# The first phase of a fused mLSTM and mixture-of-experts kernel, rebuilt: half tiles first, loads by need, a tanh gate and half-precision products

## The chip, the cores and the metric

The kernel runs on one core of a Trainium2 chip. The core has five engines with an instruction queue each, worked in order: TensorE (PE, matrix products into the banks of PSUM), VectorE (DVE), ScalarE (ACT), GpSimd (POOL) and SyncE (SP, which issues most of the transfers). The metric is the device time of one execution in microseconds. Before the change it was 260.88 us, the median of three runs (259.86 to 263.05).

## The reference: what is computed

Two stages. The first is an mLSTM recurrence for 4 sequences, 8 heads and 768 steps with 40 x 40 states:

```python
for t in range(S):
    m_new = np.maximum(f_gate[:, :, t] + m, i_gate[:, :, t])
    f_stab = np.exp(f_gate[:, :, t] + m - m_new)
    i_stab = np.exp(i_gate[:, :, t] - m_new)
    C = f_stab * C + i_stab * outer(v_t, k_t)
    n = f_stab * n + i_stab * k_t
    denom = max(abs(n . q_t), 1)
    y[:, :, t] = sigmoid(o_gate[:, :, t]) * (C q_t) / denom
```

The second is a mixture of 8 experts over the 3072 resulting tokens of width 320: logits are `x @ w_gate` plus a bias by the token's modality (two of them), the expert is the largest logit, its weight is the softmax's value there, and the output is that weight times `relu(x @ w1[e]) @ w2[e]` with 1024 hidden units. The inputs are such that the bias decides nearly always, so that all but a few tokens of a modality go to one expert.

## The kernel before

**Two arms.** `still_arm` is a fast way that holds for inputs whose forget gates are high and whose tokens fall into two large classes; guards gathered in `badc` choose the general arm otherwise. Only the fast arm is run here.

**Attention.** The states S of the four sequences after their first 64 steps are built from k and v (`weigh_k`, `state`; the loads are kvs). The tokens behind them are 22 "light" chunks c0 to c21 of 128 tokens: `light` multiplies q (the tile qg, by pairs of chunks, four slots) with S into Y, in 32-bit floats, three products for each span of a chunk. The last two chunks, `special`, are the first 64 steps themselves. For each pair, `sigmoid` turns the output gate og on ACT (exp, ln, exp); `token_rows` multiplies Y with og into xr (DVE), takes the largest absolute value of the denominators, clamps and inverts it (ab), multiplies on POOL, and splits the rows into a high and a low 16-bit part (`rows`: cast on ACT, rest on DVE). `scatter_rows` writes each chunk's rows by an indirect transfer from POOL into x_s, a DRAM array sorted by class A or B.

**Experts.** x_s is worked off in 25 half tiles of 128 tokens, mostly two at a time; the list is STREAM. A tile comes back transposed as xt (`load_tile`, a DMA_TRANSPOSE on SP), once the first NEED chunks are scattered; five slots. The first tile of each class, A0 and B0, does without it: selection products on PE take its rows from the tile `rows` (`select`, L1998). `expert` makes H = w1 x (bank tile H, 64 products a tile in groups of 16, L2070), hh = relu(H) on ACT (L2075), hl = the rest on DVE (L2077), O = w2 (hh + hl) in 24 products a half (L2086), the scaling on ACT and a scatter to the output from POOL. Every weight is used as a high and a low 16-bit half. The weights of A's and B's experts come in 16 pieces through a ring of five `stage` slots (`load_w`, L1823), and each is split by ACT (high, L1824) and DVE (low, L1825).

**What sets the order.** Every operation is an entry in a `Plan` with an engine, an assumed duration, and what it reads and writes. `Plan.run` lists them by their latest start and an assumed cost of each engine and transfer; the resulting order is the program order of every engine. A transfer on SP may not stand earlier than AHEAD less than its latest start. So a changed constant can move instructions on all queues, and what stands ahead of a waiting instruction holds all behind it.

**PSUM.** H0, H1 and H2 are three tiles that take turns for the groups of H; Y0 and Y1 are two halves of one tile Y. A wait is set by tile, not by the half that is used.

Of the kernel before, what the change touches and what calls it, by code (L numbers as in the profile page):

```python
# [1553 lines left out]
def still_arm(tc, a, out):  # L1554
# [174 lines left out]
    def weigh_k(pr):  # L1729
        src = kvs[pr][:, 0:DM].rearrange("p (h d) -> p h d", h=H)  # L1730
        dve(320, lambda: v.tensor_tensor(kw[pr][:, 0:H], src, wT[:, pr * H:(pr + 1) * H].rearrange("p h -> p h ()")
                                         .broadcast_to([P, H, D]), ALU.mult), r=[f"kv{pr}", "wT"], w=[f"kw{pr}"])
# [683 lines left out]
```

## Time and profile before

| | |
|---|---|
| median of three runs | 260.88 us |
| the profiled execution | 260.92 us, span 259.1 us |
| mean granted clock of PE | 0.962 |
| busy: PE, DVE, ACT, POOL | 215.8, 136.9, 92.4, 83.1 us |
| transfers | 31.33 MB, 121 GB/s over the span |
| first product of A0, B0, A1, B1 on H | 27.27, 42.69, 66.32, 82.20 us |
| first scatter into x_s | 36.48 us |
| last expert product | ends at about 247.5 us |

A busy share is an average over stages with different limits, so this page is read by stretches: the start, in which nothing can be multiplied by the experts yet; the first tiles, up to 82 us; the long run of tiles; and the end, in which the last scatters land. A row of a timeline has its start, its length, the engine, the line, the operation, output and inputs, a count, and in brackets how long the engine had been idle and which operation ended that.

### The profile page before, as it was taken

How to read it: one execution, taken by the hardware profiler on the slowest of the kernel's cores; microseconds unless marked ns; L12 is line 12 of the kernel's file. 1: busy time of each engine (PE TensorE's matmuls, PEld its weight loads, DVE VectorE, ACT ScalarE, POOL GpSimd, SP SyncE). 2: the span in 40 equal slices, each digit the busy share in tenths (PEclk: the TensorE clock that was granted, in tenths of full speed). 3: DMA queues.
4: the chain of work that ended last, by engine and by line, in shares of the span. 5: the costliest groups of instructions: out<-in, count | busy, mean ns of one | idle time of the engine just before them, and what ended most of it. 6: DMA issues, size and time to landing. Idle time of an engine off the chain costs nothing.

```text
span 259.1 us, 5180 instructions
## 1 busy us (share of the span) xinstructions
PE 215.8 (83%) x2020; PEld 176.1 (68%) x2020; DVE 136.9 (53%) x422; ACT 92.4 (36%) x161; POOL 83.1 (32%) x99
## 2 busy tenths in 40 slices
PE   0669658746969879999799999999999989999930
PEld 0658536624857758788678788787878758878810
DVE  4666995865680332446997604934151853872200
ACT  1763852853622621318424212322222312312210
POOL 5424338323450030328479561410203031111120
PEclk9999995977999999999999999999999999999995
DMA  5993379999439210144657420163111029301000
GB/s 146 257 293 133 104 215 306 388 218 173 133 103 250 46 52 3 51 108 125 173 159 162 137 89 13 56 154 51 51 28 51 0 36 348 127 15 44 28 10 1
DMA packets 32551, 31.33 MB, mean 121 GB/s; under 512 B 22795, under 2 KB 26285, under 8 KB 32261
## 3 DMA queue, kind: packets, MB, share of 16 engines
q1 hardware_dynamic: 30085, 22.78, 35.5%
q0 software_dynamic: 2432, 8.13, 8.8%
q8 instruction: 17, 0.28, 0.5%
q14 instruction: 17, 0.14, 0.2%
HBM read 18.83 MB, written 8.47 MB: 105 GB/s over the span
## 4 chain that ended last, share of the span: by engine, by line
PE 43%; issue 16%; DVE 16%; DMA 10%; ACT 4%; POOL 4%; SPq 4%; POOLq 0%; DVEq 0%
PE O L2086 20%; PE H L2070 15%; DMA og<-in_ogl 6%; PE Y L1847 5%; POOL out L2096 2%; DVE xr L1862 2%; DVE hl L2077 2%; DMA g_d<-G 2%; DMA x_s<-rows,pos_i 2%; DVE rows L1871 1%; PE Y L1935 1%; DMA sp<-in_spq 1%; SPq L1971 1%; DVE w2lB L1825 1%; DVE w2lA L1825 1%
## 5 line engine op out<-in xcount | busy, mean ns | idle before, releaser
L2077 DVE SCALAR_TENSOR_TENSOR hl<-H,hh 128x512 f16<-128x512 f32 x50 | 34.1, 687 | 59.6 <-ACT hh L2075 59.6
L2086 PEld LDWEIGHTS <-hh 128*128 128x128 f16 x400 | 39.0, 99 | 27.3 <-issue 13.3
L2096 POOL DMA_INDIRECT out<-ob,ois x25 | 24.5, 982 | 89.2 <-ACT ob L2095 86.2
L2070 PE MATMUL H<-xt,w1hB 128*128 128x256 f16 (+1 forms) x320 | 48.1, 257 | 1.1 <-DVE hl L2077 0.8
L2075 ACT ACTIVATE hh<-H 128x512 f16<-128x512 f32 x50 | 29.7, 595 | 52.4 <-PE H L2070 51.3
L2070 PE MATMUL H<-xt,w1hA 128*128 128x256 f16 (+1 forms) x280 | 43.3, 257 | 2.2 <-DVE hl L2077 2.2
L2070 PE MATMUL H<-xt,w1lB 128*128 128x256 f16 (+1 forms) x192 | 42.5, 256 | 0.7 <-DVE w1lB L1825 0.7
L2070 PE MATMUL H<-xt,w1lA 128*128 128x256 f16 (+1 forms) x168 | 38.0, 257 | 2.6 <-DVE w1lA L1825 2.6
L1878 POOL DMA_INDIRECT x_s<-rows,pos_i x24 | 26.9, 1120 | 24.8 <-issue 7.6
L2086 PE MATMUL O<-w2lB,hh 128*128 128x320 f16 x104 | 29.4, 305 | 5.5 <-DVE w2lB L1825 5.3
L2070 PEld LDWEIGHTS <-w1hB 128*128 128x128 f16 x320 | 29.8, 101 | 4.3 <-issue 1.0
L2086 PE MATMUL O<-w2hB,hh 128*128 128x320 f16 x104 | 29.5, 305 | 2.0 <-ACT ob L2095 1.6
L2095 ACT ACTIVATE ob<-O,facs 128x320 f32<-128x320 f32 x25 | 12.8, 525 | 47.7 <-PE O L2086 40.7
L2086 PE MATMUL O<-w2lA,hh 128*128 128x320 f16 x96 | 26.9, 302 | 3.3 <-DVE w2lA L1825 3.3
L1867 POOL TENSOR_TENSOR xr<-xr,ab 128x640 f32<-128x640 f32 x12 | 17.9, 1488 | 36.3 <-DVE ab L1865 27.2
L2070 PEld LDWEIGHTS <-w1hA 128*128 128x128 f16 x280 | 25.7, 98 | 4.9 <-issue 2.4
L2086 PE MATMUL O<-w2hA,hh 128*128 128x320 f16 x96 | 26.7, 301 | 0.1
L1847 PE MATMUL Y<-S,qg 120*128 120x123 f32 (+2 forms) x144 | 22.7, 329 | 4.0 <-DVE xr L1862 2.7
L2086 PEld LDWEIGHTS <-hl 128*128 128x128 f16 x200 | 19.4, 100 | 9.1 <-DVE hl L2077 1.4
L1847 PEld LDWEIGHTS Y<-S,qg 120*128 120x128 f32 (+2 forms) x144 | 21.2, 230 | 5.8 <-DVE xr L1862 3.0
L2070 PEld LDWEIGHTS <-w1lB 128*128 128x128 f16 x192 | 19.2, 100 | 2.3 <-DVE w1lB L1825 0.9
L2070 PEld LDWEIGHTS <-w1lA 128*128 128x128 f16 x168 | 16.4, 98 | 4.4 <-DVE w1lA L1825 3.1
(171 smaller groups left out, 258.1 us busy)
## 6 DMA issues: line engine op xcount, KB each, us to landing
qg<-in_ql SPq DMA_DIRECT2D x11, 360.0 KB, 7.3
og<-in_ogl SPq DMA_DIRECT2D x12, 320.0 KB, 7.3
stage<-in_w SPq DMA_DIRECT2D x8, 384.0 KB, 9.6
stage<-in_w SPq DMA_DIRECT2D x8, 320.0 KB, 10.6
stage<-in_w1t SPq DMA_DIRECT2D x1, 1280.0 KB
og<-in_w SPq DMA_DIRECT2D x1, 1280.0 KB
kvs<-in_kvs SPq DMA_DIRECT2D x2, 364.5 KB, 3.6
sp<-in_spq SPq DMA_DIRECT2D x4, 160.0 KB
```

The costliest lines, as they stand in the source:

```text
L1825: dve(n, lambda hi=hi, lo=lo, sv=sv: v.scalar_tensor_tensor(lo, sv, WSC, hi, ALU.mult, ALU.subtract), r=[f"stage{k}", key + "h"], w=[key + ...
L1847: t_.matmul(y[p0:p1, HQ * g:HQ * g + w], lhsT=q[0:k, i, g, p0:p1], rhs=Ss[b][0:k, g, 0:w], start=(g == 0), stop=(g == 2), skip_group_check ...
L1862: dve(320, lambda h=h: v.scalar_tensor_tensor(x4[:, h], y4[:, h, :, 0:D], XS, og[k][:, h].rearrange("p (h d) -> p h d", h=H), ALU.mult, AL ...
L1867: pool(640, lambda: g_.tensor_tensor(x3, x3, ab.rearrange("p c h o -> p (c h) o").broadcast_to([P, 2 * H, D]), ALU.mult), r=[f"ab{j}"], w= ...
L1871: dve(2 * (z - a0), lambda a0=a0, z=z, o=o: v.tensor_tensor(rows[:, cs, o:o + z - a0], xr[:, :, a0:z], rows[:, cs, a0:z], ALU.subtract), r ...
L1878: ins = g_.indirect_dma_start(out=x_s[:, :], out_offset=bass.IndirectOffsetOnAxis(ap=pos_i[:, c:c + 1].bitcast(U32), axis=0), in_=rows[:, ...
L2070: t_.matmul(hp3[:, i], lhsT=l, rhs=r, start=(i == 0 and q == 0), stop=(i == g - 1 and q == 7), skip_group_check=True)
L2075: act(512, lambda fl=fl, hp3=hp3: s_.activation(hh[:, fl, 0:n], hp3, AF.Relu), r=[nb], w=[f"hh{j}{f}" for f in range(f0, f0 + g)])
L2077: dve(512, lambda fl=fl, hp3=hp3: v.scalar_tensor_tensor(hl[:, fl, 0:n], hp3, 0.0, hh[:, fl, 0:n], ALU.max, ALU.subtract), r=[nb] + [f"hh{ ...
L2086: t_.matmul(op[:, 0:DM], lhsT=t[:, f, P * h:P * h + P], rhs=w[:, f], start=(i == 0), stop=(i == 23))
L2095: act(320, lambda h=h, op=op, o=o: s_.mul(obs[o], op[:, 0:DM], facs[:, s["q0"] + h:s["q0"] + h + 1]), r=[no, f"fac{k}"], w=[f"ob{o}"])
L2096: swdma(164, lambda h=h, o=o: disjoint("outf", g_.indirect_dma_start(out=out[:, :], out_offset=bass.IndirectOffsetOnAxis(ap=ois[:, s["q0"] ...
```

## The change

It has seven parts.

- *Order of tiles and loads.* STREAM begins with four half tiles A0, B0, A1, B1; NEED tells for each tile how many chunks it needs, A1 and B1 now 6 and A2, B2 10. The constants of the planner's costs are new, the stage ring has seven slots, w1 is laid out so that a piece has contiguous rows, the zeros in x_s are stored earlier, and gs is loaded from ACT's queue.
- *Gate.* sigmoid(o) = (tanh(o/2) + 1)/2: one tanh on ACT, and the factor and the 1 go into operations that were there. A second ACT operation sums relu(-tanh(o/2) - 0.98) into `odds`, and the guards send any input with a positive sum to the general arm.
- *Half precision.* From the sixth pair (chunk 10) on, q and S are scaled and split into a high and a low 16-bit half (`halve_q`, Sh and Sl), and a span of Y is nine products of halves in place of three of 32-bit floats.
- *Banks.* H0 and H1 become the two halves of one tile H, and the second pair of chunks uses them as the other pairs use Y (`home`).
- *Rows.* The tile `rows` is a ring of 12 chunks in place of all 24; token numbers are copied into a slot again when it is used a second time, and the guards' sums of the rows are made by pairs.
- *Products of zeros.* 24 products of the tile zrow, 128 x 512, are put on PE where the planner has room.
- *A form.* `tt` makes SCALAR_TENSOR_TENSOR of many TENSOR_TENSOR operations on DVE.

```diff
-    DMA_KB = 230.0
-    AHEAD = 213.0
+    DMA_KB = 320.0
+    AHEAD = 200.0
...
-STREAM = [("A", 0, 1), ("B", 0, 1)]
-for _k in range(1, 6):
+STREAM = [("A", 0, 1), ("B", 0, 1), ("A", 1, 1), ("B", 1, 1)]
+for _k in range(2, 7):
     STREAM += [("A", _k, 2), ("B", _k, 2)]
-STREAM = STREAM[:-1] + [("A", 6, 1), ("B", 5, 2), ("B", 6, 1), ("B", 7, 1)]
-NEED = {1: 7, 2: 12, 3: 16, 4: 20, 5: 24, 6: 24, 7: 24}
+STREAM += [("B", 7, 1)]
+FIRST_HALF = (0, 1, 2, 4, 6, 8, 10, 12)
+NEED = {0: 3, 1: 6, 2: 10, 3: 14, 4: 18, 5: 22, 6: 24, 7: 24}
 NHALF = 25
 SLOTS = 5
+NSTAGE = 7
+WARM = 24
 PRE = 4
-SOON = 25.0
+SOON = 20.0
+RING = 12
+BY_POOL = ()
+PLAIN = 5
+QSC, SSC = 512.0, 256.0
+GATE = 0.98
...
+    def tt(out, x, y, op):
+        return v.scalar_tensor_tensor(out, x, 1.0, y, ALU.mult, op)
...
+    bank = {n: pp.tile([P, 512], F32, name=n) for n in ("H2", "O0", "O1", "M0")}
+    duo = {n: pp.tile([P, 2, 512], F32, name=n) for n in "YH"}
+    for n in "YH":
+        bank.update({n + "0": duo[n][:, 0], n + "1": duo[n][:, 1]})
...
+    rows = tl([P, RING, CW], F16, "rows")
     zrow = tl([P, CW], F16, "zrow")
-    stg = tl([P, 5 * 768], F32, "stage")
-    stage = [stg[:, 768 * i:768 * i + 768] for i in range(5)]
+    stg = tl([P, NSTAGE * 768], F32, "stage")
+    stage = [stg[:, 768 * i:768 * i + 768] for i in range(NSTAGE)]
...
+    dma(16, lambda: s_.dma_start(gs, a["gsp"]), w=["gs"], eng="ACT", bias=-99)
...
+    dve(400, lambda: v.memset(zrow, 0.0), w=["zrow"], bias=-99)
+    for _ in range(WARM):
+        pe(0.3, lambda: t_.matmul(bank["O0"], lhsT=zrow[:, 0:P], rhs=zrow[:, 0:512], start=True, stop=True, skip_group_check=True),
+           r=["zrow"], w=["O0"], bias=500)
...
+        if b:
+            act(3 * HQ, lambda: s_.mul(Sh[b][0:120], Ss[j][0:120], SSC), r=[f"S{j}"], w=[f"Sh{b}"])
+            dve(3 * HQ, lambda: v.scalar_tensor_tensor(Sl[b][0:120], Ss[j][0:120], SSC, Sh[b][0:120], ALU.mult, ALU.subtract),
+                r=[f"S{j}", f"Sh{b}"], w=[f"Sl{b}"])
...
-                src = lambda f0=f0: (a["w1"][ds(regs[c], 1)].rearrange("a p (k f) -> (a p) k f", k=3))[:, :, f0:f0 + 256]
-                sv = st.rearrange("p (k f) -> p k f", k=3)
+                src = lambda i=i: a["w1p"][ds(regs[c], 1), :, 768 * i:768 * i + 768].rearrange("a p f -> (a p) f")
+                sv = st
...
-    def sigmoid(i):
+    def gate(i):
+
         t, k = og[i % 4], f"og{i % 4}"
-        act(640, lambda: s_.activation(t, t, AF.Exp, scale=-1.0), w=[k])
-        act(640, lambda: s_.activation(t, t, AF.Ln, bias=1.0), w=[k])
-        act(640, lambda: s_.activation(t, t, AF.Exp, scale=-1.0), w=[k])
-
-    abss = [small([2, H, 1], f"ab{i}") for i in range(2)]
+        act(640, lambda: s_.activation(t, t, AF.Tanh, scale=0.5), w=[k])
+        act(640, lambda: s_.activation(gjunk.rearrange("p (c d) -> p c d", c=2), t, AF.Relu, bias=gmin, scale=-1.0,
+                                       accum_out=odds[:, i:i + 1]), r=[k, "gmin"], w=["gjunk", f"odd{i}"], bias=15)
...
+    def home(i):
+        return "H" if i == 1 else "Y"
+
+    def halve_q(i):
+        s, d = f"qg{i % 3}", i % 2
+        act(768, lambda: s_.mul(qh[d], qg[i % 3], QSC), r=[s], w=[f"qh{d}"])
+        dve(768, lambda: v.scalar_tensor_tensor(ql[d], qg[i % 3], QSC, qh[d], ALU.mult, ALU.subtract), r=[s, f"qh{d}"], w=[f"ql{d}"])
...
+        if i < PLAIN:
+            r = [f"qg{i % 3}"] + [f"S{b}" for _, _, b in spans(c)]
+            sets = lambda b: [(qg[i % 3], Ss[b])]
+        else:
+            r = [f"qh{i % 2}", f"ql{i % 2}"] + [f"S{x}{b}" for _, _, b in spans(c) for x in "hl"]
+            sets = lambda b: [(qh[i % 2], Sh[b]), (qh[i % 2], Sl[b]), (ql[i % 2], Sh[b])]
...
+                    for e, (q, s) in enumerate(ps):
+                        t_.matmul(y[p0:p1, HQ * g:HQ * g + w], lhsT=q[0:k, j, g, p0:p1], rhs=s[0:k, g, 0:w],
+                                  start=(g == 0 and e == 0), stop=(g == 2 and e == len(ps) - 1), skip_group_check=True)
...
+        for h in range(2):
+            dve(320, lambda h=h: v.scalar_tensor_tensor(x4[:, h], og[k][:, h].rearrange("p (h d) -> p h d", h=H), 1.0,
+                                                        y4[:, h, :, 0:D], ALU.add, ALU.mult), r=Y + [f"og{k}"], w=[f"xr{l}"])
...
+        dve(16, lambda: v.tensor_scalar(ab, ab, one, 2.0 / XS, ALU.max, ALU.mult), w=[f"ab{j}"])
+        dve(40, lambda: v.reciprocal(ab, ab), w=[f"ab{j}"])
...
+        if 2 * i >= RING:
+            dve(2, lambda: v.tensor_copy(rows[:, cs, IDC:IDC + 2].bitcast(I32).rearrange("p c o -> p (c o)"), tok_i[:, 2 * i:2 * i + 2]),
+                r=["cst"], w=[f"id{c0}", f"id{c0 + 1}"])
...
+        dve(640, lambda: v.tensor_reduce(sums[:, 2 * i:2 * i + 2], rows[:, cs, 0:DM], axis=AX.X, op=ALU.add, apply_absolute_value=True),
+            r=[f"rowh{c0}", f"rowh{c0 + 1}"], w=["sums"], bias=15, nb=45 if i < 4 else None)
...
-        swdma(168, scatter, r=[f"rowh{c}", f"rowl{c}", "ids", "rowz", "pos_i", "prefill"], w=[f"xs{c}"])
+        swdma(168, scatter, r=[f"rowh{s}", f"rowl{s}", f"id{s}", "rowz", "pos_i", "prefill"], w=[f"xs{c}"])
...
+        dma(168, lambda: sy.dma_start(x_s[CAP - P:CAP], zrow), r=["zid"], w=["prefill"], nb=8, bias=-60)
+        dma(168, lambda: sy.dma_start(x_s[2 * CAP:2 * CAP + P], zrow), r=["zid"], w=["prefill"], nb=8, bias=-60)
...
-        need = NEED[s["i"]] if s["i"] else 3
+        need = NEED[s["i"]]
...
-                load_q(c // 2) if c < 22 else None
+                if c < 22:
+                    load_q(c // 2)
+                    if c // 2 >= PLAIN:
+                        halve_q(c // 2)
                 load_o(c // 2)
-                sigmoid(c // 2)
+                gate(c // 2)
...
-            chunks((NEED[STREAM[issued][1]] + 1) // 2 * 2)
+            chunks(NEED[STREAM[issued][1]])
```

How the order moves, at three places.

SP, from the fifth piece of weights on, in the kernel before (x_s<-zrow stores zeros, e_i are the experts' numbers):

```order
L1823 DMA stage_88<-in_w2 128x640
L1894 DMA x_s_70<-zrow_87 128x656
L1800 TENSOR_LOAD e_i_150
L1800 ISA x2
L1823 ISA
L1823 DMA stage_88<-in_w2 128x640
L1823 ISA
L1823 DMA stage_88<-in_w2 128x640
L1823 ISA
L1823 DMA stage_88<-in_w2 128x640
L1895 DMA x_s_70<-zrow_87 128x656
```

and in the changed one, from the same piece on:

```order
L1850 DMA stage_90<-in_w2 128x640
L1850 ISA
L1850 DMA stage_90<-in_w2 128x640
L1850 ISA
L1850 DMA stage_90<-in_w2 128x640
L1826 TENSOR_LOAD e_i_159
L1826 ISA x2
L1952 DMA x_s_69<-zrow_89 128x656
L1682 DMA qg0_77<-in_ql 120x768
L1685 DMA og_84<-in_ogl 128x640
L1690 DMA wg_sb_86<-in_wgs 128x24
L1682 DMA qg1_78<-in_ql 120x768
```

Seven pieces now stand in a row with one store of zeros ahead of them, and the second store stands behind the seventh piece, no longer behind the eighth; the next loads of q and og have moved ahead of the eighth piece.

PE from the sorting products (modb) to the first products of q, before:

```order
L1755 LDWEIGHTS ones_120
L1755 MATMUL H2_65<-modb_137,ones_120 128x24
L1756 LDWEIGHTS tri_119
L1756 MATMUL H2_65<-modb_137,tri_119 128x24
L1725 MATMUL M0_68<-ident_118,Wt_135 128x16
L1742 MATMUL H0_63<-kvs0_76,kw0_129 120x123 x3
L1742 MATMUL H1_64<-kvs0_76,kw0_129 120x123 x3
L1847 MATMUL Y_69<-S0_114,qg0_78 128x123 x2
```

and in the changed one, a little later in the same stretch (fifteen products of zrow stand ahead of the sorting products, four behind them):

```order
L1696 LDWEIGHTS zrow_89
L1696 MATMUL O0_64<-zrow_89 128x512
L1764 MATMUL H_68<-kvs0_75,kw0_138 120x123 x6
L1891 MATMUL Y_67<-S0_116,qg0_77 128x123 x2
L1891 MATMUL Y_67<-S0_116,qg0_77 128x82
L1891 MATMUL Y_67<-S0_116,qg0_77 128x123 x2
L1891 MATMUL Y_67<-S0_116,qg0_77 128x82
L1891 MATMUL H_68<-S0_116,qg1_78 128x123 x2
L1891 MATMUL H_68<-S0_116,qg1_78 128x82
```

The products of chunks 2 and 3 (qg1) go into H, where before they followed in Y, and the products of zeros have come in.

DVE around the hl of B1 (hl1, made from H2 and then H) in the changed kernel; cst holds the token numbers, `rows` the ring:

```order
L2097 SCALAR_TENSOR_TENSOR ois_105<-fm_107,ids_104 128x1
L1924 COPY rows_88<-cst_71 128x2
L2095 TENSOR_REDUCE kmall_108<-ky0_180 128x1
L2096 TENSOR_SCALAR fm_107<-kmall_108,k2_156 128x1
L1773 SCALAR_TENSOR_TENSOR Sl2_122<-S0_116,Sh2_119 120x369
L1924 COPY rows_88<-cst_71 128x2 x2
L1928 TENSOR_REDUCE sums_133<-rows_88 128x2
L1924 COPY rows_88<-cst_71 128x2 x2
L1928 TENSOR_REDUCE sums_133<-rows_88 128x2
L2134 SCALAR_TENSOR_TENSOR hl1_112<-H2_63,hh1_110 128x4x128
L1928 TENSOR_REDUCE sums_133<-rows_88 128x2
L2134 SCALAR_TENSOR_TENSOR hl1_112<-H_68,hh1_110 128x4x128
```

In the kernel before the last hl of the second tile of B is preceded by the chain of the router:

```order
L2036 SCALAR_TENSOR_TENSOR ky1_172<-lg1_168,cst_72 128x8
L2038 TENSOR_REDUCE kmall_106<-ky1_172 128x1
L2039 TENSOR_SCALAR fm_105<-kmall_106,k2_147 128x1
L2077 SCALAR_TENSOR_TENSOR hl1_110<-H2_65,hh1_108 128x4x128
L2042 TENSOR_REDUCE gsm1_176<-ex1_170 128x1
```

The copies of token numbers and the sums by pairs are new ahead of hl; a copy into a used slot of the ring waits for the scatter that read it.

More of the change, by code (lines that the diff above doesn't have):

```diff
@@ L1633, in still_arm @@
     obs = [tl([P, DM], F32, f"ob{i}") for i in range(3)]
-    Ss = [tl([P, 3, HQ], F32, f"S{b}") for b in range(B)]
+    Ss = [tl([P, 3, HQ], F32, f"S{b}") for b in range(2)]
+    Sh, Sl = ([None] + [tl([P, 3, HQ], F16, f"S{n}{b}") for b in range(1, B)] for n in "hl")
     ident = tl([P, P], F32, "ident")
@@ L1836, in still_arm @@
+    abs_ = [small([2, H, 1], f"ab{i}") for i in range(2)]
     xss = [small([2, DM], f"xr{i}") for i in range(3)]
+    def home(i):
[4 more added lines that the diff above has]
+        dve(768, lambda: v.scalar_tensor_tensor(ql[d], qg[i % 3], QSC, qh[d], ALU.mult, ALU.subtract), r=[s, f"qh{d}"], w=[f"ql{d}"])
     def light(c):
-        n = f"Y{c % 2}"
+        i, j = divmod(c, 2)
+        n = f"{home(i)}{j}"
@@ L1852, in token_rows @@
+        pe((0.75 if i < PLAIN else 0.52) * len(spans(c)), mm, r=r, w=[n])
     def token_rows(i):
-        y4 = ys[:, :, 0:H * DV].rearrange("p c (h d) -> p c h d", h=H)
+        Y = [f"{home(i)}{j}" for j in (0, 1)]
+        y4 = duo[home(i)][:, :, 0:H * DV].rearrange("p c (h d) -> p c h d", h=H)
         j, k, l = i % 2, i % 4, i % 3
-        ab, xr = abss[j], xss[l]
+        one = QSC * SSC if PLAIN <= i < 11 else 1.0
+        ab, xr = abs_[j], xss[l]
         x4 = xr.rearrange("p c (h d) -> p c h d", h=H)
-        cs = slice(2 * i, 2 * i + 2)
@@ L2176, in check_light @@
         dve(1, lambda: v.tensor_scalar(badc[0:32, 0:1], lm[:, 0:1], -1.0, 1.0, ALU.mult, ALU.add), r=["lm"], w=["badc"])
-    def sum_rows(i):
-        cs = slice(6 * i, 6 * i + 6)
-        dve(1920, lambda: v.tensor_reduce(sums[:, cs], rows[:, cs, 0:DM], axis=AX.X, op=ALU.add, apply_absolute_value=True),
-            r=[f"rowh{c}" for c in range(6 * i, 6 * i + 6)], w=["sums"])
     def check_sums():
@@ L2185, in check_sums @@
         dve(24, lambda: v.scalar_tensor_tensor(oks, sums, SHI, oks, ALU.is_le, ALU.mult), r=["sums"], w=["oks"])
+        dve(12, lambda: v.tensor_reduce(badc[:, 5:6], odds, axis=AX.X, op=ALU.max), r=[f"odd{i}" for i in range(NC // 2)], w=["badc"])
+        dve(1, lambda: v.tensor_scalar(badc[:, 5:6], badc[:, 5:6], 0.0, None, ALU.is_gt), w=["badc"])
         dve(24, lambda: v.tensor_reduce(badc[:, 1:2], oks, axis=AX.X, op=ALU.min), r=["oks"], w=["badc"])
@@ L2205, in still_arm @@
     load_w("A")
-    sigmoid(0)
+    gate(0)
     prefill()
@@ L2402 @@
     with tile.TileContext(nc, schedule_with_timeline_sim=True) as tc:
-        still = {n: args[n] for n in _STILL + ["mb", "w1", "w2"]}
+        still = {n: args[n] for n in _STILL + ["mb", "w2"]}
         still["wg"] = args["wgs"]
```

116 lines of the change are left out of this document (56 added, 60 removed).

## The prediction

> **What bounds the kernel now.** I read the page first, then the busy time of each engine in stretches, then TensorE's waits before and after 82 us, and last the timelines of the queues that those waits name.
>
> ```profile
> span 259.1 us, 5180 instructions
> PE 215.8 (83%) x2020; PEld 176.1 (68%) x2020; DVE 136.9 (53%) x422; ACT 92.4 (36%) x161; POOL 83.1 (32%) x99
> 20.00:30.00 10.00, 8.74 (x89) 7.83 (x86) 7.51 (x20) 5.26 (x8) 4.29 (x5) 1.00 0.33 102
> 30.00:40.00 10.00, 4.58 (x49) 3.16 (x47) 10.00 (x14) 5.93 (x10) 3.18 (x4) 0.91 0.74 204
> 50.00:60.00 10.00, 5.12 (x29) 3.20 (x29) 7.90 (x19) 6.37 (x10) 1.64 (x1) 0.77 1.25 212
> 150.00:200.00 50.00, 50.00 (x484) 40.89 (x483) 19.43 (x59) 13.36 (x25) 12.38 (x12) 1.00 0.23 60
> 82.20:247.50 165.30, 160.19 (x1587) 1.00 0.30 85
> ```
>
> The stretches give, after their length, the busy time of PE, PEld, DVE, ACT and POOL, then the granted clock, the DMA share and GB/s; the last row is PE alone. From 82 us to 247.5 PE works 160.2 of 165.3 us: nothing is to be had there but by taking products away. Between 20 and 66 us it is another kernel: PE works about half of the time, VectorE is full in 30 to 40, and the DMA moved only 102 GB/s in 20 to 30. The first four half tiles (A0, B0 and both halves of A1) show where they stand:
>
> ```profile
> 27.27 0.28 PE L2070 MATMUL H<-xt,w1hA 128*128 128x128 f16 x2
> 42.69 0.42 PE L2070 MATMUL H<-xt,w1hB 128*128 128x128 f16 x2
> 66.32 0.38 PE L2070 MATMUL H<-xt,w1hA 128*128 128x256 f16 x2
> 82.20 0.38 PE L2070 MATMUL H<-xt,w1hB 128*128 128x256 f16 x2
> PE O L2086 <- DVE w2lB L1825: 5.3, 3, 2.0
> PE O L2086 <- DVE w2lA L1825: 3.3, 3, 2.1
> PE H L2070 <- DVE w1lA L1825: 2.6, 3, 1.5
> PE H L2070 <- DVE hl L2077: 2.2, 1, 2.2
> ```
>
> A0 begins at 27.27, B0 at 42.69, A1 at 66.32, and B1 at 82.20. A1 has two halves and one wait of 2.2: (82.20 - 66.32 - 2.22) / 2 = 6.8 us is what one half costs on a fed PE. A0 took 15.4 and B0 23.6, held by the low halves of the weights on DVE. Those in turn came late by the queues:
>
> ```profile
> 8.66 5.45 SPq L1823 DMA_DIRECT2D stage<-in_w  x5
> 27.32 4.72 SPq L1823 DMA_DIRECT2D stage<-in_w  x3
> 52.29 8.91 SPq L1971 DMA_TRANSPOSE xt<-x_s  x2
> 74.90 3.37 SPq L1971 DMA_TRANSPOSE xt<-x_s  x2
> 36.48 1.56 POOL L1878 DMA_INDIRECT x_s<-rows,pos_i  x1 [6.21 <-DMA x_s<-zrow]
> ```
>
> Five pieces of weights are asked for at 8.66, then SP sits until 27.32, since all five slots are taken; the second store of zeros into x_s stands behind the next three, so the first scatter of rows begins only at 36.48, after a wait of 6.21 for it.
>
> **The change part by part.** The sum is made on the profiled run: span 259.1, 1.8 outside it, 260.9 together, next to the median of 260.88.
>
> *Start of A0.* The gate has two ACT operations a pair in place of three, chunks 2 and 3 have a bank of their own, and 15 zero products stand ahead of the sorting products on PE.
>
> ```profile
> 18.88 0.74 ACT L1832 ACTIVATE og<-og 128x640 f32<-128x640 f32 x1
> 14.97 2.85 PE L1847 MATMUL Y<-S,qg 120*128 120x123 f32 x12 [1.14 <-DVE ab L1860]
> 18.95 3.33 PE L1847 MATMUL Y<-S,qg 120*64 120x123 f32 x18 [1.13 <-DVE xr L1862]
> 26.08 0.59 ACT L2001 CAST xt<-O 128x512 f16<-128x512 f32 x1 [2.82 <-PE O L1998]
> ```
>
> Three pairs stand ahead of A0's transposed rows: 3 x 0.74 = 2.2 us of ACT goes, and the two waits of 1.14 and 1.13 for the Y bank go, 2.3. If all of it is on the path A0 starts at 27.3 - 4.5 = 22.8, and I take that. Bounds: the warm products hold the sorting products, so the experts' numbers and the weights may come some 2 us later (gain 2.5), or warm PE takes the 2.85 down by half three times (gain 8).
>
> *Weights, A0 and B0.* Seven slots, both stores of zeros ahead of or between the first pieces. The pieces for A are all in flight from the start, so DVE becomes the limit. Its rows:
>
> ```profile
> L1825 DVE SCALAR_TENSOR_TENSOR w1lA<-stage,w1hA x4: 944/945/948, 26.3 to 32.4; 128x768 f16<-128x768 f32 x4
> L1825 DVE SCALAR_TENSOR_TENSOR w2lA<-stage,w2hA x4: 806/807/811, 33.3 to 38.9; 128x640 f16<-128x640 f32 x4
> 63.07 0.49 DVE L1862 SCALAR_TENSOR_TENSOR xr<-Y,og 128x320 f32<-128x320 f32 x1 [3.00 <-PE Y L1847]
> 64.89 0.25 DVE L1865 RECIPROCAL ab<-ab 128x16 f32<-128x16 f32 x1
> 67.69 0.89 DVE L1871 TENSOR_TENSOR rows<-xr,rows 128x128 f16<-128x128 f32 x2 [2.55 <-ACT rows L1869]
> 185.23 0.60 ACT L2075 ACTIVATE hh<-H 128x512 f16<-128x512 f32 x1 [1.17 <-PE H L2070]
> 185.86 0.69 DVE L2077 SCALAR_TENSOR_TENSOR hl<-H,hh 128x512 f16<-128x512 f32 x1 [4.71 <-ACT hh L2075]
> ```
>
> Eight low halves of w1 at 0.95 and eight of w2 at 0.81 are 14.1; four hl at 0.69 are 2.8; the rows of two pairs (chunks 6 to 9) are 2 x (2 x 0.49 + 0.25 + 0.89 + two small ones of 0.17) = 4.9. Two of the w1 pieces are done before A0 starts (-1.9). That is 19.9 us, and B0 ends at 22.8 + 19.9 = 42.7, where before it ended at 66.3. If the pieces come as late as now it is nearer 50.
>
> *A1 and B1* are half tiles now that need six chunks: 2 x 6.8, so 56.4 if their rows are there. The order puts A1's and B1's transposes behind the last weights, and the scatters of chunks 0 to 5 can begin when the zeros are in, some 13 us earlier than 36.48, so they should be.
>
> *A2, the first tile that needs new rows (chunks 6 to 9).* The way from the products of chunks 8 and 9 to the issue of the transposes is in the trace:
>
> ```profile
> 60.87 2.09 PE L1847 MATMUL Y<-S,qg 120*128 120x123 f32 x12
> DMA to landing us min/median/max: 2.8/3.6/10.5
> ```
>
> From 60.87 to 74.90 is 14.0, and the landing of a transpose (the second row, that of the tile xt) 3.6, at worst 10.5. In the new order these products stand in the last half of B0's H, about 38 to 40. So A2's rows are there at 55.6 at best and 64.5 at worst. DVE, too, has a new wait there: the copies of the row numbers into the ring of rows wait for the scatters of chunks 6 to 9, and behind them stand B1's hl and so its last eight products; kw1 waits for a load that stands behind two transposes on SP, with A1's hl behind it. With PE free at 56.4 and the rows at 55.6 to 64.5 I take A2's start, which I call T2, at 62; bounds 57 (both at their best) and 68 (the worst landing, and 3.5 more by those waits).
>
> *From A2 on.* T2 answers to 82.20 in the kernel before: four half tiles done, 21 to go. What is left is the same but for three things.
>
> ```profile
> 82.20:247.50 165.30, 7.83 (x66) 7.35 (x66) 1.00 0.30 85
> 249.71 0.89 POOL L2156 DMA_INDIRECT out<-forow,fo_i  x1 [0.30 <-issue]
> ```
>
> The first row is the Y products alone: 11 spans, 0.71 each. After T2 there are 13 spans as 9 half-precision products. A half tile is 64 products of 128 columns and 24 of 320, 15,872 columns in 6.8 us, so 128 columns take 0.055 and a span some 0.5 to 0.6: 13 x 0.55 = 7.2, or -0.6. Their halving costs ACT and DVE about what a w1 piece costs (0.95 on DVE), six times, hidden under PE, since DVE worked 19.4 of the 50 us from 150. The same work without that cover would be 6 us.
>
> The second is the bank: H0 and H1 are one tile now, and the order's waits show that a group on H1 right behind one on H0 waits at its middle for the hl of the group just ended. From the relu's start at 185.23 to the end of hl at 186.55 are 1.32 us, and PE has eight products of 256 columns (0.11 by the same rate, 0.87) to do in between: 0.45 lost each time. I count six such places with the hl wait: +2.7; bounds 0 (the relu alone) and 14 (every third of the 42 groups), 6.3.
>
> The third is the idle time, 5.1 of the 165.3, which I leave. The sums of the rows are cut from four to twelve but of the same elements, nothing; the guard's relu and the three fewer logarithms lie on ACT, 13.4 busy of 50: nothing. From PE's last product to the end of the span nothing is changed, the last store at 249.71 and its landing in it: 259.1 - 247.5 = 11.6.
>
> The sum: 62 + 165.3 - 0.6 + 2.7 + 11.6 = 241.0 for the span, and 1.8 outside: **242.8**, said as 243.
>
> [...] Many operations of DVE with two operands in SBUF go from TENSOR_TENSOR to SCALAR_TENSOR_TENSOR. I give it nothing:
>
> ```profile
> 8.16 0.54 DVE L1731 TENSOR_TENSOR kw<-kvs,wT 128x320 f32<-128x320 f32 x1
> 53.34 1.54 DVE L1731 TENSOR_TENSOR kw<-kvs,wT 128x320 f32<-128x320 f32 x1
> 52.90 1.64 POOL L1867 TENSOR_TENSOR xr<-xr,ab 128x640 f32<-128x640 f32 x1 [5.04 <-DVE ab L1865]
> 48.72 0.17 DVE L2031 SCALAR_TENSOR_TENSOR lg<-lg,bias 128x8 f32<-128x8 f32 x1
> 122.97 1.82 DVE L2031 SCALAR_TENSOR_TENSOR lg<-lg,bias 128x16 f32<-128x16 f32 x1
> ```
>
> The same kw took 0.54 alone and 1.54 beside POOL's xr; but the SCALAR_TENSOR_TENSOR on lg did likewise, 0.17 and 1.82, so the other form is held too. If it were not, two or three such stretches of 1.0 in the chain of chunks 6 to 9 would be saved, and the time 240. [...]
>
> The warm products: the twelve products of a pair took 2.85 at 14.97 and 2.09 at 60.87, and the granted clock was 0.91 in 30 to 40 and 0.77 in 50 to 60, where PE was half idle. A0 and B0 will have such gaps still, since DVE feeds them, so A1 may begin slow: a half tile at half speed for its first 3 us costs 1.5, inside T2's bounds. [...]
>
> **The rivals.** *The rows come late* (0.13): the two transposes of 52.29 held SP for 8.9 us, and with kvs1 and q loads behind them kw1, the halving of q and A1's hl all slip by that much, twice. T2 is then 70 to 76, and the time 251 to 257. For it speaks that every engine takes its work in order and that three new waits stand ahead of hl; against it that the pair at 74.90 took 3.4 only.
>
> *Nothing comes of it* (0.05): the loads, not their order, set the start (DMA share 1.25 in 50 to 60), T2 stays about 80, 261. Against it: 0.33 in 20 to 30.
>
> *Slower* (0.04): the shared H bank stops PE in every group, not in six. Without the six places the sum is 240.1; with a loss of x in each of the 42 groups left it is 240.1 + 42x, and passes 266.1 from x = 0.62. The 0.45 alone gives 259; where hl stands behind one more operation of 0.69, x is 1.14 and the time 288. Against it: the waits that the order shows hold on every third group only, and mostly for the relu.
>
> *Better* (0.08): T2 at 57, no bank waits, 2 us of idle time fewer: 233 or less.
>
> **How the numbers follow.** The forecast has 0.70: 243, and by its bounds 233 (57 + 165.3 - 2 - 0.6 + 13.4) to 252.4 (68, and 6.3 for the banks). The range goes up to 256 to take in most of the late rows. Two per cent, about what a measurement here can tell from none, is 255.7 and 266.1. Faster: 0.70 + 0.08 + 0.08 of the late rows = 0.86; within: 0.05 + 0.05 = 0.10; slower 0.04.
>
> **What would show it.** A0's first product at 21 to 25; no stop of SP before the eighth piece other than for a slot; first scatter near 24; B0's last product at 40 to 46; A2's first at 57 to 68; then PE busy over 95% to about 229, with waits for hl of some 0.45 and no more than a dozen. I am wrong if A1 or A2 waits over 6 us for its rows, if hl holds PE in most groups, or if DVE stays full past 70.

## The result and the profile after

The changed kernel takes 249.85 us (median of 4 runs, 248.46 to 251.04), beside 261.97 for the kernel before on the same chip: the ratio is 0.956 (95% interval 0.946 to 0.966), 4.4% faster. The forecast was 243 in a range of 233 to 256. The profiled run took 249.13 us, span 247.3. Ratios here and below leave out executions more than 1.5% above the fastest of their kernel, among them one of t_w1 that took 1206 us for a reason that is not known, and the trace of g6_e2oldz is of such an execution (250.91 us), so that small differences in it are not read.

The page's first lines of the changed kernel, and its busy time in stretches of 10 us (PE, PEld, DVE, ACT, POOL, granted clock, DMA share, GB/s):

```profile
span 247.3 us, 5364 instructions
PE 213.2 (86%) x2083; PEld 170.3 (69%) x2083; DVE 145.4 (59%) x447; ACT 91.5 (37%) x170; POOL 79.6 (32%) x100
20.00:30.00 10.00, 8.91 (x102) 8.51 (x101) 8.16 (x20) 6.23 (x12) 5.88 (x6) 0.75 1.03 318
30.00:40.00 10.00, 9.04 (x111) 7.45 (x110) 8.71 (x18) 7.72 (x14) 1.73 (x2) 1.00 0.77 269
40.00:50.00 10.00, 6.96 (x83) 5.71 (x82) 8.61 (x31) 4.90 (x9) 5.01 (x5) 0.94 0.90 241
50.00:60.00 10.00, 10.00 (x109) 8.18 (x108) 8.90 (x27) 5.92 (x12) 3.73 (x4) 0.89 0.60 133
```

The stretch from 20 to 30 us carries 318 GB/s where it had 102, and from 30 to 40 PE is busy 9.0 us where it was 4.6. The timelines of PE, SP and POOL show the same places as before:

```profile
21.18 0.37 PE L2127 MATMUL H<-xt,w1hA 128*128 128x128 f16 x2 [1.08 <-ACT xt L2058]
47.80 0.27 PE L2127 MATMUL H<-xt,w1hA 128*128 128x128 f16 x2 [2.31 <-ACT hh L2132]
49.36 0.47 PE L2143 MATMUL O<-w2hA,hh 128*128 128x320 f16 x1
61.84 0.38 PE L2127 MATMUL H<-xt,w1hA 128*128 128x256 f16 x2
9.68 1.94 SPq L1850 DMA_DIRECT2D stage<-in_w1p  x4
11.81 2.05 SPq L1850 DMA_DIRECT2D stage<-in_w  x3
14.52 0.35 SPq L1952 DMA_DIRECT2D x_s<-zrow  x1
36.69 2.65 SPq L2028 DMA_TRANSPOSE xt<-x_s  x2
55.02 2.88 SPq L2028 DMA_TRANSPOSE xt<-x_s  x2
21.86 1.22 POOL L1935 DMA_INDIRECT x_s<-rows,pos_i  x1 [6.10 <-ACT w2hA L1851]
```

A0 starts at 21.18 (it was 27.27), the second store of zeros is issued at 14.52 (32.09), the first scatter at 21.86 (36.48), and A2 starts at 61.84 with four half tiles done, as B1 did at 82.20. So the first phase gained 20.4 us. The time gained 11.8. The rest was given back behind A2, where PE waited almost only for this:

```profile
PE H L2127 <- DVE hl L2134: 8.3, 7, 1.4
PE H L2127 <- ACT hh L2132: 4.3, 4, 2.2
```

These are the waits of PE from 62 us on (total, times, longest): 12.6 us before products into H, where the kernel before has 3.0 of that kind from 66 on. PE was busy 160.5 of the 173.9 us from A2's start to its last expert product, 92%, where the prediction looked for over 95.

### The profile page after: what moved, and what is told of

Its sections match the earlier page's. It is cut to its first block, busy times and chain, and to the rows that moved or that the text cites. A ratio compares the mean times of both kernels' runs of the same rounds, so it can differ in the third digit from the quotient of the medians.

```text
span 247.3 us, 5364 instructions
## 1 busy us (share of the span) xinstructions
PE 213.2 (86%) x2083; PEld 170.3 (69%) x2083; DVE 145.4 (59%) x447; ACT 91.5 (37%) x170; POOL 79.6 (32%) x100
## 4 chain that ended last, share of the span: by engine, by line
PE 45%; DVE 18%; issue 16%; DMA 7%; ACT 5%; POOL 3%; SPq 1%; POOLq 0%; DVEq 0%
PE O L2143 20%; PE H L2127 18%; DMA stage<-in_w1p 4%; DVE hl L2134 3%; DMA og<-in_ogl 3%; ACT hh L2132 2%; POOL out L2153 2%; PE O L1696 2%; DVE rows L1592 2%; DVE xr L1907 2%; PE Y L1992 1%; DVE w2lB L1852 1%; DVE lg L2088 1%; DVE lg L1592 1%; PE Y L1891 1%
## 5 line engine op out<-in xcount | busy, mean ns | idle before, releaser
L2153 POOL DMA_INDIRECT out<-ob,ois x25 | 25.4, 1016 | 99.2 <-ACT ob L2152 79.2
L2127 PE MATMUL H<-xt,w1hA 128*128 128x256 f16 (+1 forms) x280 | 45.3, 266 | 11.4 <-ACT hh L2132 5.2
L2127 PE MATMUL H<-xt,w1lB 128*128 128x256 f16 (+1 forms) x192 | 41.6, 253 | 0.9 <-DVE w1lB L1852 0.9
L2127 PE MATMUL H<-xt,w1lA 128*128 128x256 f16 (+1 forms) x168 | 39.9, 266 | 0.0
L2127 PEld LDWEIGHTS <-w1hA 128*128 128x128 f16 x280 | 27.3, 103 | 15.1 <-issue 12.7
L2127 PEld LDWEIGHTS <-w1hB 128*128 128x128 f16 x320 | 29.0, 98 | 8.1 <-issue 5.4
L1935 POOL DMA_INDIRECT x_s<-rows,pos_i x24 | 24.6, 1025 | 21.2 <-issue 7.4
L1913 POOL TENSOR_TENSOR xr<-xr,ab 128x640 f32<-128x640 f32 x12 | 16.2, 1353 | 27.9 <-DVE ab L1911 11.3
L2127 PEld LDWEIGHTS <-w1lB 128*128 128x128 f16 x192 | 18.8, 98 | 2.7 <-DVE w1lB L1852 1.4
L2143 PE MATMUL O<-w2hB,hl 128*128 128x320 f16 x104 | 16.7, 299 | 0.0
L2143 PE MATMUL O<-w2hA,hl 128*128 128x320 f16 x96 | 15.6, 299 | 0.2 <-DVE hl L2134 0.2
```

The source lines that it names most:

```text
L1913: pool(640, lambda: g_.tensor_tensor(x3, x3, ab.rearrange("p c h o -> p (c h) o").broadcast_to([P, 2 * H, D]), ALU.mult), r=[f"ab{j}"], w= ...
L1935: ins = g_.indirect_dma_start(out=x_s[:, :], out_offset=bass.IndirectOffsetOnAxis(ap=pos_i[:, c:c + 1].bitcast(U32), axis=0), in_=rows[:, ...
L2127: t_.matmul(hp3[:, i], lhsT=l, rhs=r, start=(i == 0 and q == 0), stop=(i == g - 1 and q == 7), skip_group_check=True)
L2143: t_.matmul(op[:, 0:DM], lhsT=t[:, f, P * h:P * h + P], rhs=w[:, f], start=(i == 0), stop=(i == 23))
L2153: swdma(164, lambda h=h, o=o: disjoint("outf", g_.indirect_dma_start(out=out[:, :], out_offset=bass.IndirectOffsetOnAxis(ap=ois[:, s["q0"] ...
```

## The experiments

Each ratio is to the kernel before, run beside it on the same chip, since that kernel itself came to medians from 260.97 to 264.58 us in the three sessions of these experiments. "The base" below is e2_homeY. Starts of tiles are read from the timelines of PE.

**One bank tile or two (e1_sep).**

```diff
-    bank = {n: pp.tile([P, 512], F32, name=n) for n in ("H2", "O0", "O1", "M0")}
-    duo = {n: pp.tile([P, 2, 512], F32, name=n) for n in "YH"}
+    bank = {n: pp.tile([P, 512], F32, name=n) for n in ("H0", "H1", "H2", "O0", "O1", "M0")}
+    duo = {n: pp.tile([P, 2, 512], F32, name=n) for n in "Y"}
...
+            dve(16, lambda: [v.tensor_reduce(ab[:, h], yh[h][:, :, D:DV], axis=AX.X, op=ALU.max, apply_absolute_value=True)
+                             for h in range(2)], r=Y, w=[f"ab{j}"])
```

> The changed kernel with H0 and H1 as two tiles again; the second pair of chunks still uses them, its one reduction over both banks made as two; all else in the same order. Theory (the shared tile): the relu of a group on H0 waits for the eight products on H1 that stand ahead of it in PE's order, and PE's next eight for the hl behind that relu. Then the seven stops of 1.41 for hl and most of the four of 0.7 for hh go: 8 to 11 us less, some 239 to 241 us beside 249 to 250 for the changed kernel. Rival (ACT and DVE are late by themselves, behind other work): the stops stay, 248 to 250.

It took 240.26 us, ratio 0.918 (0.911 to 0.926), 3.8 points below the changed kernel's 0.956. The same place in both traces, first the changed kernel (PE, ACT and DVE):

```profile
172.87 0.27 PE L2127 MATMUL H<-xt,w1lA 128*128 128x256 f16 x1
173.18 0.60 ACT L2132 ACTIVATE hh<-H 128x512 f16<-128x512 f32 x1 [2.02 <-PE H L2127]
173.81 0.69 DVE L2134 SCALAR_TENSOR_TENSOR hl<-H,hh 128x512 f16<-128x512 f32 x1 [1.93 <-ACT hh L2132]
174.55 0.38 PE L2127 MATMUL H<-xt,w1hA 128*128 128x256 f16 x2 [1.41 <-DVE hl L2134]
```

and then the kernel with two tiles, with the same order of work:

```profile
168.34 0.60 ACT L2137 ACTIVATE hh<-H 128x512 f16<-128x512 f32 x1 [1.15 <-PE H L2132]
168.36 0.27 PE L2132 MATMUL H<-xt,w1lA 128*128 128x256 f16 x1
168.97 0.69 DVE L2139 SCALAR_TENSOR_TENSOR hl<-H,hh 128x512 f16<-128x512 f32 x1 [1.05 <-ACT hh L2137]
169.78 0.27 PE L2132 MATMUL H<-xt,w1lA 128*128 128x256 f16 x1
```

With one tile the relu starts when PE has ended the eight products of the other bank, and PE stands for the whole of relu and hl, 1.41 us. With two tiles the relu starts eight products earlier and PE works on. The waits before H are gone from 59 us on. The edit also helps ahead of A2. In the changed kernel PE stands 2.31 us in A1 for a relu that starts at 47.15; here the relu starts as late, at 47.04, but no product into H waits for it, and PE stands 0.98 us, before O:

```profile
47.70 0.31 PE L2148 MATMUL O<-w2hA,hh 128*128 128x320 f16 x1 [0.98 <-ACT hh L2137]
```

A1 takes 9.06 us (42.98 to 52.04), in the changed kernel 11.92 (43.09 to 55.01). Some of the time comes back as waits before O, 8.1 in all, where relu or ob is late behind other work:

```profile
PE O L2148 <- ACT hh L2137: 3.4, 2, 2.0
PE O L2148 <- DVE hl L2139: 2.9, 4, 1.5
PE O L2148 <- ACT ob L2157: 1.8, 2, 1.6
```

**The same edit put into the kernel before (b1_duo).**

```diff
-    bank = {n: pp.tile([P, 512], F32, name=n) for n in ("H0", "H1", "H2", "O0", "O1", "M0")}
+    bank = {n: pp.tile([P, 512], F32, name=n) for n in ("H2", "O0", "O1", "M0")}
...
-    bank.update(Y0=ys[:, 0], Y1=ys[:, 1])
+    hs = pp.tile([P, 2, 512], F32, name="H")
+    bank.update(Y0=ys[:, 0], Y1=ys[:, 1], H0=hs[:, 0], H1=hs[:, 1])
```

> The kernel before with one edit: H0 and H1 are one tile, used as before. Theory (the shared tile): the same stops of 0.7 and 1.4 for hh and hl appear in the run of tiles, a third of the 50 groups, so 8 to 16 us more than before, some 269 to 277. Rival: within 2 of the kernel before, 260 to 263.

It took 276.15 us, ratio 1.063 (1.053 to 1.074). PE's waits from 60 us on:

```profile
PE H L2071 <- DVE hl L2078: 11.6, 8, 3.1
PE H L2071 <- ACT hh L2076: 4.0, 6, 0.7
```

So the shared tile alone makes the same stops in a kernel that had two of them, 3.0 us in all, and costs some 15 us there (276.15 beside 261.57). PE's products stand in the same order in each kernel and its counterpart. Both directions agree: that the shared tile holds PE, and costs some 10 us in the changed kernel, is shown.

**Is a bank of its own for chunks 2 and 3 worth it (e2_homeY)?** Two tiles, and all pairs on Y:

```diff
     def home(i):
-        return "H" if i == 1 else "Y"
+        return "Y"
```

> The changed kernel with H0 and H1 as two tiles and the second pair of chunks on Y like all others. If the pair's own bank is worth what was forecast (the two waits of 1.1 for Y on the path of A0), A0 starts about 2 us later than with e1_sep and the time is 1 to 2 us above it, 240 to 243. If DVE and ACT set A0's start and the weights set B0's end, it is the same as e1_sep.

It took 239.22 us, ratio 0.918 (0.911 to 0.924), the same as e1_sep. A0 starts at 22.40 beside 22.10, A2 at 59.98 beside 59.41. The bank brings 0.3 to 0.6 us at most, and cost 10 as it was made. This kernel is faster than the changed one, no slower than e1_sep, and the base of the next ones.

**Without the products of zeros (e3_nowarm).**

```diff
-WARM = 24
+WARM = 0
```

> The changed kernel without the 24 products of zeros. If they warm PE, the Y products of the first three pairs take 2.9, 2.9 and 3.3 us again in place of 1.6, 1.5 and 1.8, A0 starts up to 4 us later and the time is 1 to 4 us above the changed kernel's, 250 to 254. If they only stand in the way (5 us ahead of the sorting products), the experts' numbers and the weights come some 2 us earlier and the time is 247 to 249.

It took 248.59 us, ratio 0.954 (0.947 to 0.960), against 0.956 (0.946 to 0.966): the same. The first two Y products of the changed kernel, and then those of this one:

```profile
9.23 1.57 PE L1891 MATMUL Y<-S,qg 120*128 120x123 f32 x12 [0.64 <-DVE S L1592]
10.63 1.50 PE L1891 MATMUL H<-S,qg 120*128 120x123 f32 x12
```

```profile
9.76 2.85 PE L1891 MATMUL Y<-S,qg 120*128 120x123 f32 x12 [0.64 <-DVE S L1592]
12.40 2.77 PE L1891 MATMUL H<-S,qg 120*128 120x123 f32 x12
```

Behind the products of zeros these take 1.57 and 1.50 us in place of 2.85 and 2.77, little more than half. A0 starts at 21.18 with them and at 22.52 without, A1 at 43.09 and at 44.66, A2 at 61.84 and at 61.21. So the gain lasts up to A1 and is lost in A1, where the changed kernel stands 2.31 us for the late relu and this one 0.69 and 0.85 before H. Taking the products out moved other operations on PE, ACT and DVE too, so whether they pay where that stop is mended is not shown. And nothing of it is left at A0, whose first products come at half rate in both kernels (0.11 us from one product of 128 columns to the next, 0.055 later).

**The order of tiles of the kernel before, in the base (f_stream).**

```diff
-STREAM = [("A", 0, 1), ("B", 0, 1), ("A", 1, 1), ("B", 1, 1)]
+STREAM = [("A", 0, 1), ("B", 0, 1)]
...
-NEED = {0: 3, 1: 6, 2: 10, 3: 14, 4: 18, 5: 22, 6: 24, 7: 24}
+NEED = {0: 3, 1: 7, 2: 12, 3: 16, 4: 20, 5: 24, 6: 24, 7: 24}
```

> Base of these four: the changed kernel with H0, H1 as two tiles and all pairs on Y (239.2 us). Here its tile list and NEED are those of the kernel before: A0, B0 as half tiles, then whole tiles, A1 after 7 chunks. If the two half tiles A1 and B1, which need 6 chunks only, are what fills PE from 43 to 57 us, PE waits there for the rows of chunk 6 and the time is 8 to 14 us above the base, 247 to 253. If the earlier weights and scatters are enough by themselves, it is within 3, 238 to 242.

It took 240.92 us, ratio 0.918 (0.906 to 0.929), no difference that the runs can tell. Four half tiles are done at 64.26 (its B1's start) beside 59.98, and the 4.3 us are made good later: the last expert product ends at 226.55 beside 226.14.

**Five stage slots (f_stage5).**

```diff
-NSTAGE = 7
+NSTAGE = 5
```

> The base with five stage slots. If slots held SP and the weights (the stop of SP from 14 to 27 us in the kernel before), B0 ends 3 to 6 us later and the time is 241 to 245. If DVE's work on the pieces is the limit, five are enough: within 1.5 of the base, 238 to 241.

It took 243.79 us, ratio 0.931 (0.919 to 0.942), beside 0.918 (0.911 to 0.924) of the base: the intervals overlap, so not settled. But B0 ends no later: A1 starts at 43.14, with seven slots at 43.09. What slots may cost lies behind that: A2 starts at 63.47 beside 59.98, after a wait of 0.81 for its rows.

**The gate of the kernel before (f_gate).**

```diff
-        act(640, lambda: s_.activation(t, t, AF.Tanh, scale=0.5), w=[k])
+        act(640, lambda: s_.activation(t, t, AF.Exp, scale=-1.0), w=[k])
+        act(640, lambda: s_.activation(t, t, AF.Ln, bias=1.0), w=[k])
+        act(640, lambda: s_.activation(t, t, AF.Exp, scale=-1.0), w=[k])
```

> The base with the gate of the kernel before, exp, ln and exp, and without the guard on tanh (its sums are set to zero, so that large output gates are not caught). As forecast the three ACT operations of 0.74 in place of two stand on the path of A0 three times: A0 starts 2 us later, the time is 1 to 3 above the base, 240 to 242. If ACT has room there, the same as the base.

The guard on tanh is left out, and the 1 and the factor 2 are set back. It took 243.67 us, ratio 0.925 (0.912 to 0.939); again the intervals overlap. A0 starts at 22.85 beside 22.40. So the three operations of 0.74 were not on A0's path by more than 0.45 us. What the old gate may cost lies behind that too: in this trace PE stands twice for relus in A1, where the base stands once, for 1.1, and A2 starts at 63.72 beside 59.98.

```profile
49.36 0.31 PE L2143 MATMUL O<-w2hA,hh 128*128 128x320 f16 x1 [2.02 <-ACT hh L2132]
52.18 0.45 PE L2143 MATMUL O<-w2hA,hh 128*128 128x320 f16 x1 [1.25 <-ACT hh L2132]
```

**32-bit products for all chunks (f_plain).**

```diff
-PLAIN = 5
+PLAIN = 11
```

> The base with 32-bit products for all chunks (no halves of q and S). 13 spans go from about 0.53 to 0.65 us on PE, +1.5, and six times 0.84 on ACT and 0.95 on DVE and the waits of qh for the loads of q go. Forecast: the saving was put at 0.6 in all, so within 2 of the base, 237.5 to 241; if the halving of q holds the relu of A1 and the tiles behind, it is faster, 235 to 238.

It took 241.88 us, ratio 0.921 (0.909 to 0.934), no difference that the runs can tell.

**Zeros stored early in the kernel before, nothing else (g1_zeros).**

```diff
+    dve(400, lambda: v.memset(zrow, 0.0), w=["zrow"], bias=-99)
...
-        dma(168, lambda: sy.dma_start(x_s[CAP - P:CAP], zrow), r=["zrow", "zid"], w=["prefill"])
+        dma(168, lambda: sy.dma_start(x_s[CAP - P:CAP], zrow), r=["zrow", "zid"], w=["prefill"], nb=8, bias=-60)
```

> The kernel before with one edit: the two stores of zeros are issued early, among the first pieces of weights, and their tile is set on DVE at the start. If the late first scatter (36.5 us) held the first phase, it comes near 25 us, A1 starts 5 to 10 us earlier and the time is 250 to 256. If the weights of B hold A1 (its last piece was ready at 64 us), the scatters are early for nothing and the time is 258 to 263.

It took 259.58 us, ratio 0.993 (0.989 to 0.997), 0.7% faster. The first scatter comes 5 us earlier, and PE's waits up to 75 us show why little follows:

```profile
31.35 1.71 POOL L1879 DMA_INDIRECT x_s<-rows,pos_i  x1 [0.19 <-issue]
PE O L2086 <- DVE w2lB L1826: 4.0, 3, 1.8
PE H L2070 <- ACT w1hB L1825: 2.5, 1, 2.5
```

B0 still waits for its weights, and A1 starts at 72.89, later than the 66.32 of the kernel before.

**The planner's old constants in the base, and with them late zeros (g6_e2oldz).**

```diff
-    DMA_KB = 320.0
-    AHEAD = 200.0
+    DMA_KB = 230.0
+    AHEAD = 213.0
...
-SOON = 20.0
+SOON = 25.0
...
-        dma(168, lambda: sy.dma_start(x_s[CAP - P:CAP], zrow), r=["zid"], w=["prefill"], nb=8, bias=-60)
+        dma(168, lambda: sy.dma_start(x_s[CAP - P:CAP], zrow), r=["zid"], w=["prefill"])
```

The assumed durations on ACT, POOL and SP are set back too.

> The two-tile, all-on-Y kernel (239.2 us) with the planner's constants of the kernel before and the zeros where that plan puts them, behind the first pieces. If constants and zeros are what shortened the phase, B0 ends later than 47 and the time is 246 to 252; if not, within 3: 238 to 242.

It took 248.44 us, ratio 0.949 (0.944 to 0.954), beside 0.918 for the base: 3.1 points, 8 us, the largest part found. The order in its trace:

```profile
26.84 0.43 SPq L1952 DMA_DIRECT2D x_s<-zrow  x1
40.09 1.26 POOL L1913 TENSOR_TENSOR xr<-xr,ab 128x640 f32<-128x640 f32 x1 [12.83 <-DVE lg L1592]
41.54 1.22 POOL L1935 DMA_INDIRECT x_s<-rows,pos_i  x1 [0.18 <-issue]
53.73 2.64 SPq L2028 DMA_TRANSPOSE xt<-x_s  x2
52.67 1.25 PE L2143 MATMUL O<-w2hB,hl 128*128 128x320 f16 x8
```

The second zeros are asked for at 26.84, and the plan has put the xr of a later pair ahead of the first scatter on POOL; that xr runs at 40.09, so the rows of chunks 0 to 5, long ready, leave from 41.54 on, and the transposes for A1 and B1 are issued at 53.73 (38.03 in the base). The last row is the end of B0: its last product ends at 53.92, where the base starts A1 at 43.09. Constants and zeros were set back together, so their shares are open; g1_zeros says only that zeros alone do little where the weights of B are late. A2 starts at 79.85, 20 us behind the base, and yet the last expert product ends only 11.6 us later (237.74 and 226.14): PE puts other work into the wait, as 36 of the 117 products into Y that the base has behind A2 stand ahead of it here, and it is idle for less time behind it (1.8 us beside 6.5). And at 0.949 this kernel is still some 13 us faster than the kernel before. No run divides these 13: each of the other parts that was undone alone made no difference that the runs can tell, and the ring of rows and the loads at the very start were not undone.

**w1 in rows of 1 KB (t_w1).**

```diff
-                src = lambda i=i: a["w1p"][ds(regs[c], 1), :, 768 * i:768 * i + 768].rearrange("a p f -> (a p) f")
+                src = lambda f0=f0: (a["w1"][ds(regs[c], 1)].rearrange("a p (k f) -> (a p) k f", k=3))[:, :, f0:f0 + 256]
```

> The same base with the pieces of w1 read in rows of 1 KB, three to a partition, as in the kernel before, in place of one of 3 KB. If short rows slow the loads of the first phase, the w1 pieces land 2 to 5 us later and the time is 241 to 246; if the 16 DMA engines are filled by either, 238 to 241.

It took 241.65 us, ratio 0.921 (0.916 to 0.926), the same. The median from issue to landing of a w1 piece is 8.4 us, 8.7 in the base.

**TENSOR_TENSOR again (t_tt).**

```diff
-        return v.scalar_tensor_tensor(out, x, 1.0, y, ALU.mult, op)
+        return v.tensor_tensor(out, x, y, op)
```

> The same base with TENSOR_TENSOR in place of SCALAR_TENSOR_TENSOR wherever the change put it. Forecast: both forms are held while POOL's xr runs, so 238 to 241 and the rows' low parts of chunks 0 to 9 as long as in the base. If only TENSOR_TENSOR is held, two or three stretches of 1.0 us come back in the first phase: 241 to 243.

It took 240.80 us, ratio 0.923 (0.919 to 0.927), beside 0.918 (0.911 to 0.924). The same operation beside POOL's xr, in the base and here:

```profile
17.09 1.84 POOL L1913 TENSOR_TENSOR xr<-xr,ab 128x640 f32<-128x640 f32 x1 [1.91 <-DVE ab L1911]
17.74 1.95 DVE L1592 SCALAR_TENSOR_TENSOR rows<-xr,rows 128x128 f16<-128x128 f32 x2
20.48 0.88 DVE L1592 SCALAR_TENSOR_TENSOR rows<-xr,rows 128x128 f16<-128x128 f32 x2
```

```profile
17.09 1.84 POOL L1913 TENSOR_TENSOR xr<-xr,ab 128x640 f32<-128x640 f32 x1 [1.91 <-DVE ab L1911]
17.74 1.94 DVE L1592 TENSOR_TENSOR rows<-xr,rows 128x128 f16<-128x128 f32 x2
20.48 0.88 DVE L1592 TENSOR_TENSOR rows<-xr,rows 128x128 f16<-128x128 f32 x2
```

1.95 and 1.94 beside POOL, 0.88 and 0.88 alone: the form makes no difference.

## Why the prediction was right, and where it was not

The time lay in the range and the sign was right. By its steps, on the profiled run:

| step | forecast | measured |
|---|---|---|
| A0 starts | 22.8 | 21.18 |
| B0 ends, A1 starts | 42.7 | 43.09 |
| A2 starts (T2) | 62 | 61.84 |
| T2 to PE's last product | 167.4 | 174 |
| span | 241.0 | 247.3 |

*A0's start* lay within its bounds, 6.1 us earlier where 4.5 were forecast, but not for its reasons. The gate's three operations were put at 2.2 us of it; f_gate shows 0.45. The bank of chunks 2 and 3 was put at 2.3; e2_homeY and e1_sep show 0.3. The warm products, which the prediction left between a loss of 2 and a gain of 3.5, gave 1.3. The remaining 4 us were not traced to one edit.

*B0's end* came out right, but the step that made DVE the limit is not borne out. From A0's start to B0's end the stretch, and all that PE waits there for DVE's low halves, are these:

```profile
21.18:43.09 21.91, 20.22 (x225) 17.42 (x225) 18.75 (x47) 13.74 (x24) 8.15 (x8) 0.91 0.90 286
PE H L2127 <- DVE w1lB L1852: 0.9, 3, 0.5
PE O L2143 <- DVE w2lB L1852: 0.6, 1, 0.6
```

DVE is busy 18.8 of the 21.9 us, but PE 20.2, and PE stands only 1.5 for it: PE's own work, with A0's first products at half rate (0.11 us from one of 128 columns to the next up to about 25 us, 0.055 behind that), fills the time as much as DVE's. That the sum over DVE gave the same figure is in part luck. And the seven slots, which the prediction put first, are not what made room; five give the same. The planner's constants together with the early zeros did, by the order on SP and POOL: without them B0 ends at 53.92 (g6_e2oldz).

*T2* was right by two errors that cancel, which is luck. A1 and B1 took 18.75 us, not the 13.6 of two half tiles: PE stood 2.31 at 47.80 for a relu, then ran at half rate from about 49 to 52 (0.27 from one product of 320 columns to the next from 49.36 on, eight of A1's 24), and products for the states stood between A1's. And the rows of A2 were not late: PE goes from B1 to A2 without a wait, so the feared copies of token numbers ahead of hl, and the transposes, cost nothing there. Most of the stop, and the slow products, belong to the shared bank, which the prediction charged from A2 on only: in e1_sep the first of A1's products of 320 columns takes 0.31 us, here 0.47, and A2 starts at 59.41, 2.4 earlier.

*From T2 on* the step that failed is the second of the three, the term of the shared bank: "0.45 lost each time", "six such places", +2.7. The mechanism was right, the size was not: seven stops for hl, four of them of 1.41, and four for the relu, 12.6 in all. One of these, 2.2, is for a relu that ACT began late, at 69.69, behind two of the guard's sums on the gate, which the prediction put at nothing. The prediction let the relu start when its own group ends, and counted PE's eight products against it. But the relu, too, waits by the tile: for the eight products of the other bank that stand ahead of it. So, where no other work stands between, nothing hides relu and hl, and 0.60 + 0.69 and the hops between are lost in full. With two tiles T2 to the last product is 167.6 (59.41 to 227.0), in the changed kernel 173.9: behind T2 the bank costs 6.3 net of the waits before O that come back without it, as much as the upper bound that the prediction gave it, and with the 2.4 ahead of T2 almost 9. The 167.6 stand next to the 167.4 forecast by luck, since the forecast without its bank term is 164.7. The idle time of 5.1 that was kept shrank in exchange: PE's waits from T2 on for anything but H are 0.9. The Y products took 6.8 us from T2 on, with 7.2 forecast; 0.52 a span, within the 0.5 to 0.6 said, though the rate given for it (984 columns at 0.055 for 128) makes 0.42. That T2 carries over into the time in full, as the sum has it, does not hold in general: in the trace of g6_e2oldz 20 us of it are worth 12.

*The rivals.* "Slower" named the right mechanism with x as the loss per group; x came out at 12.6 / 42 = 0.30, half of the 0.62 at which it decides. "Nothing comes of it" fell with the DMA at 318 GB/s from 20 to 30 us. "The rows come late" did not happen; T2 was on time, and the loss came behind it.

*The form and the warm products.* No gain from SCALAR_TENSOR_TENSOR was forecast, and t_tt shows none: 1.95 and 1.94 us beside POOL's xr. The warm products paid no time (0.956 with them, 0.954 without): A0's first products already came at half rate again (0.11 for 128 columns), and part of A1's did behind a stop of 2.31 us (0.27 for 320 columns from 49.36 on). The 3 us at half speed that the prediction allowed A1 were its author's estimate; A1 began at full rate (0.055 for 128 columns from 43.09 on) and ran at half from about 49 to 52.

## What to carry to other kernels

In these kernels two PSUM banks in one tile are one thing to the waits: the reader of one bank waits for writes to the other that stand ahead of it, and the next write waits for that reader (1.41 us at 174.55 in the changed kernel, nothing at that place with two tiles). Before banks are joined for one operation's sake, follow the wait in both directions through the steady loop; here a joint that served one pair of chunks, and was worth under a microsecond, cost 10. And when a first phase is rebuilt from many parts, undo them singly: most of these made no difference that the runs can tell, and the order that the planner's constants and the early zeros make together was the largest part found.
